# Writing each 256-column product as two runs of 128 columns, one in each half of its PSUM bank

## The chip, the core and the metric

The kernel runs on one core of one Trainium2 chip. The metric is the device time of one execution in microseconds (us), where lower is better. Five engines work side by side and wait for each other through semaphores: PE (TensorE; its weight loads are listed apart as PEld), DVE (VectorE), ACT (ScalarE), POOL (GpSimd), and SP, from which most transfers are issued.

## The reference

The input x has 2048 tokens of 512 features. It is normalised by rows, then goes through a Fourier mixing branch and a two-layer network, and the two are multiplied:

```python
xn = _layernorm(x)
a = einsum("bsd,ed->bse", xn, dft_hid_re);  b = einsum("bsd,ed->bse", xn, dft_hid_im)
s = einsum("ts,bse->bte", dft_seq_re, a) - einsum("ts,bse->bte", dft_seq_im, b)
h = relu(einsum("bsd,df->bsf", xn, w1) + b1) ** 2        # 512 -> 1792
g = silu(einsum("bsf,fd->bsd", h, w2) + b2)              # 1792 -> 512
return x + s * g
```

All data are float32.

## The kernel before, in words

**Numbers.** Every float32 operand is split into a high and a low part of type fp32r (`split`, L125 on ACT and L128 on DVE), and each product of two tiles is three matmuls: high by high, high by low, low by high (`PASSES`).

**Blocks.** Matrices are cut into 2x2 blocks, and a block product is done with seven products in place of eight (`PRODUCTS`); the sums of blocks that this needs are made on DVE. The seven products are added up either inside PSUM (units, below) or by DVE when they leave it (`combine`, L306).

**PSUM.** There are eight banks of 512 float32 columns on 128 partitions. A tile from `bank` is one whole bank.

**Stages, in order of time.**

- *Plain part of the Fourier mixing's first stage* (`products`, L340): matmuls with 512 moving columns, whose output fills a bank from column 0 to 511.
- *The rest of that stage* (`mm`, L325): 48 steps of seven products, 2016 matmuls with 256 moving columns. The moving operand lies in the buffers `ga` and `gb`, the weights in `xc0` to `xc7`. The output of a matmul goes to two runs of 128 columns, one in each half of the bank: the bank is seen as `p (i d t)` with i=2, d=2, t=128, and a matmul writes all of i and t at one d. The matmul for d=0 writes columns 0 to 127 and 256 to 383, the one for d=1 the rest.
- *y's second stage* (`YUnit`, L705): 8 units of seven products of 12 matmuls, 672 in all. It multiplies by the hidden-dimension matrices.
- *MLP1* (`HUnit`, L705): 28 units of seven products of 6 matmuls, 1176 in all.
- *MLP2* (`outer`, L811): 28 steps of seven products of 6 matmuls, 1176 in all: four token chunks (c) of seven steps (p). The moving operand W2[p] lies in `wd1`, `ga`, `gb`, `xc2`, `xc3`, `xc0`, `xc1` for p = 0 to 6; the weights g come from `xc6`, `xc7` and `xc4`, the last of them from `wd0`.

**A unit** of the y stage or of MLP1 has four regions, A to D, each the first 256 columns of a bank of its own (`region`, L702). Products 1 and 2 add up in A; ACT copies A with the sign turned into B after product 1 (`seed`), where 6, 5 and 3 are added; B goes likewise into C after product 6, where product 4 is added; 7 stands alone in D. ACT takes D, A and the last state of B out (`m7`, `c11`, `c12`), DVE takes B and C out (`c22`, `c21`). Products of one unit are placed between those of the unit before, so that PE has others to do while a region is read.

**In MLP2** the 256 columns of the two token halves i=0 and i=1 go to columns 0 to 255 and 256 to 511 of the product's bank. DVE adds the seven banks of a chunk up with `combine` (for the last chunk with `step` at the end of the program), ACT writes the bias into three banks ahead (`bias`).

**Order.** The order of instructions on each engine is that of the program text (the scheduling is manual), with small tables (`Y_SIDE`, `H_SIDE`, `O_SIDE`, `EARLY`) that say between which products the loads, sums and splits of later operands are recorded. Neither order nor tables are touched here. Most loads are issued from SP, the stores of h and y from ACT's queue.

Of the kernel before, what the change touches and what calls it, by code (L numbers as in the profile page):

```python
# [10 lines left out]
AF = mybir.ActivationFunctionType  # L11
ALU = mybir.AluOpType

P = 128
S, D, F = 2048, 512, 1792
# [72 lines left out]
HI, LO = 0, 1  # L88
# [23 lines left out]
H_SLOT = {S3: 0, S1: 1, S2: 2, S4: 3, A12: 4, A11: 5, A22: 6}  # L112

C21, C11, C22, C12 = range(4)
# [5 lines left out]
def fnet_gated_kernel(ctx, tc, x, xt, ct, wd, w1, w2, b1, b2, out):  # L120
    nc = tc.nc
# [12 lines left out]
    def copy(to, src, scale=1.0):  # L134
        nc.scalar.activation(to, src, AF.Copy, scale=scale)
# [5 lines left out]
    b1s = pool.tile([P, NF], F32, name="b1s")  # L141
    b2s = pool.tile([P, D], F32, name="b2s")
# [12 lines left out]
    def bank(tag, name):  # L155

        return acc.tile([P, 512], F32, tag=tag, name=name)
# [8 lines left out]
    def halves(ap):  # L166
        return ap.rearrange("p (a b) -> p a b", a=2)


    XC = [buf(f"xc{j}", [P, 7, 2, 256], f"xc{j}", F32R) for j in range(NJ)]  # L170

# [122 lines left out]
            for q, v in ((slice(0, 3), slice(1, 4)), (slice(3, 7), slice(4, 8))) if apart else ((slice(0, 7), slice(1, 8)),):  # L294
                split(g[:, HI, q], g[:, LO, q], u[:, v])

    def combine(part_, ms):

        for to, m, frm, op in ((C21, 1, None, None), (C11, 2, C21, ALU.add), (C22, 6, C21, ALU.add),
                               (C21, 7, C22, ALU.subtract), (C12, 5, C22, ALU.subtract), (C22, 5, C21, ALU.add),  # L300
                               (C12, 3, C12, ALU.add), (C21, 4, C21, ALU.subtract)):
            m = ms[m].rearrange("p (i n) -> p i n", i=2)
            if frm is None:
                copy(part_(to), m)
            else:
                nc.vector.tensor_tensor(part_(to), m, part_(frm), op=op)  # L306
            yield
# [11 lines left out]

    def mm(ps, w, mv, first, last):  # L320

        ps = ps.rearrange("p (i d t) -> p d i t", i=2, d=2)
        for d in range(2):
            for a_, b_ in PASSES:
                nc.tensor.matmul(ps[:, d], w[:, a_, d * P:(d + 1) * P], halves(mv(b_)),  # L325
                                 start=first and d == 0 and (a_, b_) == (HI, HI),
                                 stop=last and (a_, b_) == (LO, HI), skip_group_check=True)
# [216 lines left out]
    for n, s in enumerate(steps):  # L544
# [5 lines left out]
        for p in FIRST if j == 0 and c > PLAIN else ORDER:  # L550
# [4 lines left out]
            a, b = PRODUCTS[p]  # L555
# [16 lines left out]
        if j == NJ - 1:  # L572
            e = buf("e", [P, 2048], f"c{c}")
# [9 lines left out]
    xT, W1, W2, fin, ready = {}, {}, {}, {}, {}  # L583
# [105 lines left out]
    class Unit:  # L689
# [5 lines left out]
        def region(self, k):  # L695
            if k not in self.at:
                tag = ("bb", "b20", "ba", "b21"), ("bc", "b30", "b32", "b31")
                self.at[k] = bank(tag[self.n % 2]["ABCD".index(k)], f"r{self.n}_{k}")[:, 0:256]
            return self.at[k]

        def products(self, *ks):
            for k in ks:  # L702
                ops = list(self.operands(PRODUCTS[k]))
                for i, (w, mv) in enumerate(ops):
                    nc.tensor.matmul(self.region(REGION[k]), w, mv, start=i == 0 and k in (1, 7),  # L705
                                     stop=i == len(ops) - 1, skip_group_check=True)

        def seed(self, to, frm):
            copy(self.region(to), self.region(frm), -1.0)

        def m7(self):
            copy(self.out(C21), self.region("D"))

        def c22(self):
            nc.vector.tensor_tensor(self.out(C22), self.region("B"), self.out(C21), op=ALU.add)  # L715

        def c21(self):
            nc.vector.tensor_tensor(self.out(C21), self.region("C"), self.out(C21), op=ALU.subtract)

    class YUnit(Unit):  # L720

# [11 lines left out]
            return self.y[:, k in (C21, C22), (k in (C12, C22)) * 256:][:, 0:256]  # L733

        def c11(self):
            copy(self.out(C11), self.region("A"))

        def square(self):
            pass

        def c12(self):
            copy(self.out(C12), self.region("B"))
            n = 2 * self.n * P
            nc.scalar.dma_start(Y[n // TC][n % TC:n % TC + 2 * P].rearrange("(h p) e -> p h e", h=2), self.y)

# [2 lines left out]
    class HUnit(Unit):  # L748
# [14 lines left out]
            nc.scalar.activation(to, frm, AF.Relu, bias=b1s[:, f:f + 1])  # L763

        def c11(self):
            self.relu(self.out(C11), self.region("A"), 0)

        def c12(self):
            self.relu(self.out(C12), self.region("B"), 0)
            if self.n in ACT_PAIR:  # L770
                self.relu(self.out(LOWER), self.out(LOWER), 1)

        def lower(self, to, frm, op):
            f = 2 * (self.n % NP) + 1
            nc.vector.scalar_tensor_tensor(self.out(to), self.region(frm), b1s[:, f:f + 1], self.out(C21),
                                           op0=ALU.add, op1=op)

        def c22(self):
# [18 lines left out]
    BIASED = {2: 0, 5: 1, 4: 0}  # L797

    def bias(m, n, cols=slice(0, 2)):

        m = m.rearrange("p (k e) -> p k e", k=2)[:, cols]
        b = BIASED[n] * 256
        copy(m, b2s[:, None, b:b + 256].to_broadcast([P, cols.stop - cols.start, 256]))

    def outer(m, k, n, cols=(0, 1)):

        p = n % NP
        a, b = PRODUCTS[k]
        for i in cols:
            for a_, b_ in PASSES:  # L810
                nc.tensor.matmul(m[:, i * 256:(i + 1) * 256], ready[n][:, a_, H_SLOT[a], i * P:(i + 1) * P],  # L811
                                 W2[p][:, b_, b], start=p == 0 and i == 0 and (a_, b_) == (HI, HI) and k not in BIASED,
                                 stop=p == NP - 1 and (a_, b_) == (LO, HI), skip_group_check=True)


# [161 lines left out]
    for n in range(NTC * NP):  # L977
        c, p = divmod(n, NP)
        last = c == NTC - 1
        if n and not last and p == 0:  # L980

            ms = Banks(c)
            for k in (2, 4, 5):
                bias(ms[k], k)
        elif last and p == 0:

            ms = {k: bank(t, f"m{k}_last") for k, t in
                  {1: "b20", 2: "b21", 6: "b30", 7: "b31", 5: "bb", 3: "ba"}.items()}
            m4 = bank("bc", "m40_last"), bank("b32", "m41_last")
            bias(ms[5], 5)  # L990
            bias(m4[0], 4, slice(0, 1))
            bias(ms[2], 2)
            bias(m4[1], 4, slice(1, 2))

        def add(k, p):
            if last and k == 4:
                for i in range(2):
                    outer(m4[i], k, NP * c + p, (i,))
            else:
                outer(ms[k], k, NP * c + p)  # L1000

        go(*O_SIDE.get(n, ((), ()))[0])
        if n == 1:
            for k, i in ((1, 1), (2, 1), (6, 1), (4, 1), (5, 0), (3, 0), (7, 1), (5, 1), (3, 1)):
                add(k, i)
        elif n and (not last or p < REST):
            for k in ORDER if p else FIRST_LAST if last else FIRST:
                add(k, p)
        if n == 1:

            nc.scalar.activation(stats[:, 0, 0, 0:1], stats[:, 0, 0, 0:1], AF.Silu)
        if not n:
            go("h2")
        go(f"h{n + 3}")
        if p == NP - 1 and not last:
            e = buf("e", [P, 4, 512], f"z{c}")
            list(combine(lambda k: halves(e[:, k]), ms))
            done_next = c, e
        if c and not last and p in (3, 4):
            put(*done, p - 1)  # L1020
        go(*[f"h{n + 2}"][:n], *O_SIDE.get(n, ((), ()))[1], f"h{n + 6}")
        if p == (3 if last else 5):
            load_fin(c)
        if p == NP - 1 and not last:
            done = done_next
        elif c:
            for k in ((2, 3), (0,), (1,), (), (), (), ())[p] if not last else ((), (0,), (1,), (2,), (3,), (), ())[p]:
                finish(*done, k)
# [1 line left out]

    e = buf("u", [P, 4, 512], f"z{c}")
    tail = NP - 1
    whole = slice(0, 512)
    w = [slice(i * 256, (i + 1) * 256) for i in range(2)]

    def rest(ks, ps=range(REST, NP)):
        for k in ks:
            for f in ps:
                add(k, f)

    def step(to, a, b, op, w=whole):
        nc.vector.tensor_tensor(e[:, to, w], a[:, w], e[:, b, w], op=op)

    for f in range(REST, tail - 1):
        rest((1, 2, 6, 7, 5), (f,))
    rest((1, 2), (tail - 1,))
    rest((1, 2), (tail,))
    nc.scalar.activation(e[:, C21], ms[1], AF.Copy)
    step(C11, ms[2], C21, ALU.add)
    silu(e, C11)  # L1050
    for f in (tail - 1, tail):
# [3 lines left out]
    add_x(c, e, C11)  # L1055
    step(C21, ms[7], C12, ALU.subtract)
    rest((5,), (tail - 1, tail))
    for i in range(2):
        nc.vector.tensor_tensor(m4[i][:, w[i]], m4[i][:, w[i]], e[:, C21, w[i]], op=ALU.subtract)
    step(C22, ms[5], C21, ALU.add)  # L1060
    silu(e, C22)
    step(C12, ms[5], C12, ALU.subtract)
# [8 lines left out]
    for i, part_ in enumerate((one, two)):  # L1071
        for f in range(REST, NP):
            outer(m4[i], 4, NP * c + f, (i,))
        nc.scalar.activation(e[:, C21, w[i]], m4[i][:, w[i]], AF.Silu)
        times(c, e, C21, part_)
        plus(c, e, C21, part_)

# [42 lines left out]
```

## Time and profile before

| what | before |
|---|---|
| time, median of 3 runs (lowest to highest) | 702.24 us (702.05 to 703.04) |
| the profiled execution's own time | 701.75 us |
| its span, first to last instruction | 700.0 us |
| mean granted TensorE clock over the span | 0.998 |
| ACT busy | 357.9 us (51%), 475 instructions |
| HBM traffic over the span | 214 GB/s |

The views that the prediction shows are the page's busy times, its clock row, groups of instructions by line, the chain of waits in order of time, and windows. In a group's row stand the line, engine and operation, then output<-inputs, then shapes; behind the count x, the busy time of the group in us and the mean length of one in ns. Since matmuls overlap, the length of one (280 ns) isn't the time that each adds. That time is read from the chain of waits: a row there has its start in us, its length in us, the engine, the tile, the line and how many instructions it holds, and rows don't overlap, so length by count is what one matmul added. In a window's row stand the two ends, the length, and for each engine the busy us in it with the count of instructions, then the granted clock, the share of DMA and GB/s.

### The profile page before, as it was taken

How to read it: one execution, taken by the hardware profiler on the slowest of the kernel's cores; microseconds unless marked ns; L12 is line 12 of the kernel's file. 1: busy time of each engine (PE TensorE's matmuls, PEld its weight loads, DVE VectorE, ACT ScalarE, POOL GpSimd, SP SyncE). 2: the span in 40 equal slices, each digit the busy share in tenths (PEclk: the TensorE clock that was granted, in tenths of full speed). 3: DMA queues.
4: the chain of work that ended last, by engine and by line, in shares of the span. 5: the costliest groups of instructions: out<-in, count | busy, mean ns of one | idle time of the engine just before them, and what ended most of it. 6: DMA issues, size and time to landing. Idle time of an engine off the chain costs nothing.

```text
span 700.0 us, 13144 instructions
## 1 busy us (share of the span) xinstructions
PE 693.0 (99%) x5440; PEld 670.1 (96%) x5440; DVE 605.6 (87%) x849; ACT 357.9 (51%) x475; POOL 6.4 (1%) x9
## 2 busy tenths in 40 slices
PE   8999999999999999999999999999999999999997
PEld 5778889999999999999999999999999999999997
DVE  7999769999999898788899788899748689989896
ACT  4436544435343343435455358777778764444451
POOL 0000000000000000000000000000000000101000
PEclk9999999999999999999999999999999999999999
DMA  8535756768486754367488457587426956767745
GB/s 298 198 104 197 257 202 219 257 204 290 158 294 211 259 210 166 121 239 274 151 287 280 151 185 287 195 322 266 154 118 197 388 168 188 194 197 195 227 155 157
DMA packets 51723, 150.82 MB, mean 215 GB/s; under 512 B 4944, under 2 KB 19536, under 8 KB 50256
## 3 DMA queue, kind: packets, MB, share of 16 engines
q1 hardware_dynamic: 44096, 129.80, 54.9%
q10 hardware_dynamic: 6208, 18.88, 6.8%
q0 software_dynamic: 1360, 1.31, 1.5%
q8 instruction: 42, 0.69, 0.4%
q14 instruction: 17, 0.14, 0.1%
HBM read 101.98 MB, written 47.99 MB: 214 GB/s over the span
## 4 chain that ended last, share of the span: by engine, by line
PE 94%; DVE 3%; DMA 1%; ACT 1%; issue 1%; SPq 0%; DVEq 0%; ACTq 0%
PE m L325 33%; PE m_o L811 15%; PE r_B L705 13%; PE r_A L705 8%; PE pq_b L340 8%; PE r_C L705 4%; PE r_D L705 4%; PE m_last L811 4%; PE pq_ba L340 2%; PE pq_bc L340 1%; PE pq_bb L340 1%; DMA rows<-rows 1%; DVE yg L128 0%; DMA x<-in_x 0%; DVE bn L185 0%
## 5 line engine op out<-in xcount | busy, mean ns | idle before, releaser
L325 PEld LDWEIGHTS m<-g,xc 128*128 128x128 f32 x2016 | 235.7, 188 | 0.6 <-DVE g L128 0.2
L325 PE MATMUL m<-g,xc 128*128 128x256 f32 x2016 | 236.2, 280 | 0.0
L125 ACT ACTIVATE g<-u 128x1792 fp32r<-128x1792 f32 (+3 forms) x70 | 100.1, 1431 | 143.2 <-PE m L325 47.7
L128 DVE TENSOR_TENSOR g<-u,g 128x1792 fp32r<-128x1792 f32 (+3 forms) x70 | 117.5, 1679 | 23.3 <-ACT g L125 23.1
L811 PE MATMUL m_o<-w,g 128*128 128x256 f32 x882 | 105.7, 282 | 0.0
L811 PEld LDWEIGHTS m_o<-w,g 128*128 128x128 f32 x882 | 105.5, 191 | 0.0
L125 ACT ACTIVATE g<-hr 128x1792 fp32r<-128x1792 f32 (+2 forms) x31 | 47.9, 1556 | 47.2 <-PE m_o L811 25.2
L705 PE MATMUL r_B<-xT,w 128*128 128x256 f32 x504 | 69.4, 282 | 0.0
L340 PE MATMUL pq_b<-g,xc 128*128 128x512 f32 x240 | 66.7, 397 | 1.1 <-ACT xc L125 1.0
L705 PEld LDWEIGHTS r_B<-xT,w 128*128 128x128 f32 x504 | 64.1, 190 | 0.0
L128 DVE TENSOR_TENSOR g<-hr,g 128x1792 fp32r<-128x1792 f32 (+2 forms) x31 | 56.7, 1837 | 7.1 <-ACT g L125 7.1
L340 PEld LDWEIGHTS pq_b<-g,xc 128*128 128x128 f32 x240 | 43.8, 188 | 13.9 <-ACT xc L125 3.1
L705 PE MATMUL r_A<-xT,w 128*128 128x256 f32 x336 | 44.7, 282 | 0.0
L705 PEld LDWEIGHTS r_A<-xT,w 128*128 128x128 f32 x336 | 42.1, 190 | 0.0
L705 PE MATMUL r_B<-wdp,yg 128*128 128x256 f32 x288 | 37.5, 283 | 0.2 <-DVE y L715 0.2
L705 PEld LDWEIGHTS r_B<-wdp,yg 128*128 128x128 f32 x288 | 35.6, 190 | 0.6 <-DVE y L715 0.4
L811 PE MATMUL m_last<-w,g 128*128 128x256 f32 x294 | 35.1, 282 | 0.0
L811 PEld LDWEIGHTS m_last<-w,g 128*128 128x128 f32 x294 | 35.1, 190 | 0.0
L257 DVE TENSOR_TENSOR u<-u 128x512 f32<-128x512 f32 x48 | 32.8, 684 | 1.7 <-DMA u<-in_ct 1.7
L128 DVE TENSOR_TENSOR yg<-yraw,yg 128x1792 fp32r<-128x1792 f32 x13 | 26.2, 2021 | 5.4 <-ACT yg L125 5.4
L306 DVE TENSOR_TENSOR c<-m,c 128x512 f32<-128x512 f32 x42 | 27.2, 684 | 1.7 <-PE m L325 1.0
L125 ACT ACTIVATE yg<-yraw 128x1792 fp32r<-128x1792 f32 x13 | 22.1, 1699 | 7.2 <-DVE yraw L266 5.5
(180 smaller groups left out, 862.7 us busy)
## 6 DMA issues: line engine op xcount, KB each, us to landing
u<-in_ct SPq DMA_DIRECT2D x63, 512.0 KB, 3.7
hd<-h ACTq DMA_DIRECT2D x28, 512.0 KB, 4.8
hr<-hd SPq DMA_DIRECT2D x28, 512.0 KB, 3.9
wdp<-wdd SPq DMA_DIRECT2D x8, 896.0 KB, 7.2
yraw<-pqd SPq DMA_DIRECT2D x13, 512.0 KB, 5.0
pqd<-c SPq DMA_DIRECT2D x6, 1024.0 KB, 4.4
w<-w1d SPq DMA_DIRECT2D x6, 896.0 KB, 8.7
y<-y ACTq DMA_DIRECT2D x8, 512.0 KB, 4.1
```

The costliest lines, as they stand in the source:

```text
L125: nc.scalar.activation(hi, src, AF.Copy)
L128: nc.vector.tensor_tensor(lo, src, hi.bitcast(F32), op=ALU.subtract)
L257: nc.vector.tensor_tensor(t[:, 0:2], r[:, 0:1].to_broadcast([P, 2, 256]), r[:, 1:3], op=ALU.add)
L306: nc.vector.tensor_tensor(part_(to), m, part_(frm), op=op)
L325: nc.tensor.matmul(ps[:, d], w[:, a_, d * P:(d + 1) * P], halves(mv(b_)), start=first and d == 0 and (a_, b_) == (HI, HI), stop=last and ( ...
L340: nc.tensor.matmul(accs[c][k], w, part[c, j][:, b_, 2 * h:2 * h + 2], start=j == 0 and h == 0 and (a_, b_) == (HI, HI), stop=j == NJ - 1 a ...
L705: nc.tensor.matmul(self.region(REGION[k]), w, mv, start=i == 0 and k in (1, 7), stop=i == len(ops) - 1, skip_group_check=True)
L811: nc.tensor.matmul(m[:, i * 256:(i + 1) * 256], ready[n][:, a_, H_SLOT[a], i * P:(i + 1) * P], W2[p][:, b_, b], start=p == 0 and i == 0 an ...
```

## The change

Matmuls of y's second stage, of MLP1 and of MLP2 write their 256 columns in the way that L325 does. A helper `spread` gives the view of a bank with its two halves (i), two places in each (k) and 128 columns (t). A unit's region is place k=0: columns 0 to 127 and 256 to 383 of its bank. In MLP2 token half i=0 takes place 0 and i=1 place 1. All that reads or writes these banks follows: copies, seeds, sums, biases and activations see the same 256 or 512 numbers as two or four runs of 128. Buffers in SBUF keep their layout (`halves`, `packed`). `mm` uses `spread` too, for the view it had.

```diff
+    def spread(m):
+        return m.rearrange("p (i k t) -> p k i t", i=2, k=2)
+    def packed(z):
+        return z.rearrange("p (k i t) -> p k i t", k=2, i=2)
...
-    def combine(part_, ms):
+    def combine(part_, ms, view=halves):
...
-            m = ms[m].rearrange("p (i n) -> p i n", i=2)
+            m = view(ms[m])
...
-        ps = ps.rearrange("p (i d t) -> p d i t", i=2, d=2)
+        ps = spread(ps)
...
-                self.at[k] = bank(tag[self.n % 2]["ABCD".index(k)], f"r{self.n}_{k}")[:, 0:256]
+                self.at[k] = spread(bank(tag[self.n % 2]["ABCD".index(k)], f"r{self.n}_{k}"))[:, 0]
...
-                    nc.tensor.matmul(self.region(REGION[k]), w, mv, start=i == 0 and k in (1, 7),
+                    nc.tensor.matmul(self.region(REGION[k]), w, halves(mv), start=i == 0 and k in (1, 7),
...
-            copy(self.out(C21), self.region("D"))
+            copy(halves(self.out(C21)), self.region("D"))
...
-            nc.vector.tensor_tensor(self.out(C22), self.region("B"), self.out(C21), op=ALU.add)
+            x_ = halves(self.out(C21))
+            nc.vector.tensor_tensor(halves(self.out(C22)), self.region("B"), x_, op=ALU.add)
...
-        m = m.rearrange("p (k e) -> p k e", k=2)[:, cols]
+        m = spread(m)[:, cols]
...
-                nc.tensor.matmul(m[:, i * 256:(i + 1) * 256], ready[n][:, a_, H_SLOT[a], i * P:(i + 1) * P],
-                                 W2[p][:, b_, b], start=p == 0 and i == 0 and (a_, b_) == (HI, HI) and k not in BIASED,
+                nc.tensor.matmul(spread(m)[:, i], ready[n][:, a_, H_SLOT[a], i * P:(i + 1) * P],
+                                 halves(W2[p][:, b_, b]), start=p == 0 and i == 0 and (a_, b_) == (HI, HI) and k not in BIASED,
...
-            list(combine(lambda k: halves(e[:, k]), ms))
+            list(combine(lambda k: packed(e[:, k]), ms, spread))
...
-    def step(to, a, b, op, w=whole):
-        nc.vector.tensor_tensor(e[:, to, w], a[:, w], e[:, b, w], op=op)
+    def step(to, a, b, op):
+        nc.vector.tensor_tensor(packed(e[:, to]), spread(a), packed(e[:, b]), op=op)
```

The other edits do the same to `c21`, `c11`, `c12`, `lower` and to the last chunk's copies, subtractions and activation.

No instruction is added, removed or moved on any engine. PE's order at a product of MLP1, before (the regions are r_A to r_D, xT is the moving operand, w the weights):

```order
L705 MATMUL r_A<-xT_5010,w_5_4626 128x256 x3
L705 MATMUL r_A<-xT_5206,w_5_4626 128x256 x3
L705 MATMUL r_A<-xT_5010,w_6_4535 128x256 x3
L705 MATMUL r_A<-xT_5206,w_6_4535 128x256 x3
L705 MATMUL r_B<-xT_5010,w_5_4626 128x256 x3
```

The same rows with the change, whose line number is 7 higher:

```order
L712 MATMUL r_A<-xT_5010,w_5_4626 128x2x128 x3
L712 MATMUL r_A<-xT_5206,w_5_4626 128x2x128 x3
L712 MATMUL r_A<-xT_5010,w_6_4535 128x2x128 x3
L712 MATMUL r_A<-xT_5206,w_6_4535 128x2x128 x3
L712 MATMUL r_B<-xT_5010,w_5_4626 128x2x128 x3
```

Only the shape of the output has changed, from one run of 256 to two of 128.

More of the change, by code (lines that the diff above doesn't have):

```diff
@@ L711, in m7 @@
         def m7(self):
-            copy(self.out(C21), self.region("D"))
+            copy(halves(self.out(C21)), self.region("D"))
         def c22(self):
-            nc.vector.tensor_tensor(self.out(C22), self.region("B"), self.out(C21), op=ALU.add)
+            x_ = halves(self.out(C21))
+            nc.vector.tensor_tensor(halves(self.out(C22)), self.region("B"), x_, op=ALU.add)
         def c21(self):
-            nc.vector.tensor_tensor(self.out(C21), self.region("C"), self.out(C21), op=ALU.subtract)
+            x_ = halves(self.out(C21))
+            nc.vector.tensor_tensor(x_, self.region("C"), x_, op=ALU.subtract)
     class YUnit(Unit):
@@ L735, in c11 @@
         def c11(self):
-            copy(self.out(C11), self.region("A"))
+            copy(halves(self.out(C11)), self.region("A"))
         def square(self):
@@ L741, in c12 @@
         def c12(self):
-            copy(self.out(C12), self.region("B"))
+            copy(halves(self.out(C12)), self.region("B"))
             n = 2 * self.n * P
@@ L765, in c11 @@
         def c11(self):
-            self.relu(self.out(C11), self.region("A"), 0)
+            self.relu(halves(self.out(C11)), self.region("A"), 0)
         def c12(self):
-            self.relu(self.out(C12), self.region("B"), 0)
+            self.relu(halves(self.out(C12)), self.region("B"), 0)
             if self.n in ACT_PAIR:
@@ L774, in lower @@
             f = 2 * (self.n % NP) + 1
-            nc.vector.scalar_tensor_tensor(self.out(to), self.region(frm), b1s[:, f:f + 1], self.out(C21),
+            nc.vector.scalar_tensor_tensor(halves(self.out(to)), self.region(frm), b1s[:, f:f + 1], halves(self.out(C21)),
                                            op0=ALU.add, op1=op)
@@ L799, in bias @@
     def bias(m, n, cols=slice(0, 2)):
-        m = m.rearrange("p (k e) -> p k e", k=2)[:, cols]
+        m = spread(m)[:, cols]
         b = BIASED[n] * 256
-        copy(m, b2s[:, None, b:b + 256].to_broadcast([P, cols.stop - cols.start, 256]))
+        copy(m, halves(b2s[:, b:b + 256])[:, None].to_broadcast([P, cols.stop - cols.start, 2, P]))
     def outer(m, k, n, cols=(0, 1)):
@@ L1032, in fnet_gated_kernel @@
     tail = NP - 1
-    whole = slice(0, 512)
-    w = [slice(i * 256, (i + 1) * 256) for i in range(2)]
     def rest(ks, ps=range(REST, NP)):
@@ L1047, in fnet_gated_kernel @@
     rest((1, 2), (tail,))
-    nc.scalar.activation(e[:, C21], ms[1], AF.Copy)
+    copy(packed(e[:, C21]), spread(ms[1]))
     step(C11, ms[2], C21, ALU.add)
@@ L1057, in fnet_gated_kernel @@
     rest((5,), (tail - 1, tail))
+    left = [spread(m4[i])[:, i] for i in range(2)]
     for i in range(2):
-        nc.vector.tensor_tensor(m4[i][:, w[i]], m4[i][:, w[i]], e[:, C21, w[i]], op=ALU.subtract)
+        nc.vector.tensor_tensor(left[i], left[i], packed(e[:, C21])[:, i], op=ALU.subtract)
     step(C22, ms[5], C21, ALU.add)
@@ L1073, in fnet_gated_kernel @@
             outer(m4[i], 4, NP * c + f, (i,))
-        nc.scalar.activation(e[:, C21, w[i]], m4[i][:, w[i]], AF.Silu)
+        nc.scalar.activation(packed(e[:, C21])[:, i], left[i], AF.Silu)
         times(c, e, C21, part_)
```

## The prediction

> **What bounds the kernel now.** I read the page's busy times and clock first, then what PE waited for, then the chain of waits.
>
> ```profile
> PE 693.0 (99%) x5440; PEld 670.1 (96%) x5440; DVE 605.6 (87%) x849; ACT 357.9 (51%) x475; POOL 6.4 (1%) x9
> ...
> PEclk9999999999999999999999999999999999999999
> ...
> PE 94%; DVE 3%; DMA 1%; ACT 1%; issue 1%; SPq 0%; DVEq 0%; ACTq 0%
> ...
> PE warm L443 <- DVE idle L439: 1.2, 1, 1.2
> PE pq_b L340 <- ACT xc L125: 1.0, 1, 1.0
> PE r_B L705 <- DVE y L715: 0.2, 1, 0.2
> ```
>
> PE is busy 99% of the span at a full clock, 94% of the chain that ended last is PE, and PE waited 2.4 us in all. So the time is the number of matmuls by what each adds, and the question is whether the change alters that. The chain of waits in order of time gives it (start, length, matmuls), in stretches where nothing but matmuls stands on it:
>
> ```profile
> 109.97 31.03 PE m L325 x266
> 184.88 30.22 PE m L325 x259
> 595.10 10.02 PE m_o L811 x85
> 605.35 19.68 PE m_o L811 x164
> 630.19 9.90 PE m_o L811 x84
> ```
>
> Those are stretches asked for one by one; the next rows are of the whole chain.
>
> ```profile
> 53.26 2.10 PE pq_b L340 x9
> ...
> 356.38 2.87 PE r_B L705 x24
> ...
> 396.51 2.87 PE r_B L705 x24
> ...
> 430.85 1.44 PE r_B L705 x12
> ...
> 545.97 1.44 PE r_B L705 x12
> ...
> 557.37 103.11 PE m_o L811 x864
> 660.48 27.15 PE m_last L811 x228
> ```
>
> L325 already writes in two runs: 31.03/266 = 116.7 ns a matmul, and 30.22/259 = 116.7 again. The three stages that the change touches write one run of 256 columns, with the same shapes, and are slower:
>
> - y's second stage: units of 84 matmuls begin alike at 356.38 and, four units on, at 396.51: 40.13 us/336 = 119.4 ns.
> - MLP1: units of 42 begin alike at 430.85 and, 23 on, at 545.97: 115.12/966 = 119.2 ns. The stretches shown run at 1.44/12 = 120.0.
> - MLP2: 103.11/864 = 119.3, and 27.15/228 = 119.1 for the last chunk. Within it, 19.68/164 = 120.0 and 10.02/85 = 9.90/84 = 117.9.
>
> So 3024 of the 5440 matmuls take 2 to 3 ns more than L325's. The groups say that this isn't one bad place: the mean lengths differ too, for weight loads and matmuls.
>
> ```profile
> L325 PEld LDWEIGHTS m<-g,xc 128*128 128x128 f32 x2016 | 235.7, 188 | 0.6 <-DVE g L128 0.2
> L325 PE MATMUL m<-g,xc 128*128 128x256 f32 x2016 | 236.2, 280 | 0.0
> L811 PE MATMUL m_o<-w,g 128*128 128x256 f32 x882 | 105.7, 282 | 0.0
> L811 PEld LDWEIGHTS m_o<-w,g 128*128 128x128 f32 x882 | 105.5, 191 | 0.0
> ```
>
> **The change part by part.** *The matmuls.* 672 + 1176 + 1176 = 3024 get the output view of L325; nothing else about them changes. Whether the view is what makes L325 faster must be argued, since L325 also reads other buffers. The best comparison is inside the trace. MLP2's steps p=1 and p=2 take the moving operand from `ga` and `gb` and the weights from `xc` tiles, which is where L325 has them. A step is 42 matmuls, so the second chunk's p=1 and p=2 are the 84 matmuls from 595.1, the third's those from 630.2: 117.9 ns. Same buffers, same sizes, one run instead of two: 1.2 ns more than 116.7. The steps behind them, p=3 to p=6, take the moving operand from `xc` tiles as well: 120.0. So about 1.2 ns of the 3.3 stands against the write pattern with the buffers held alike, and 2.1 goes with where the moving operand lies. What two runs do at 120.0 no row shows. The bounds: they remove nothing there, or they bring all matmuls to 116.7. Against a gain beyond the 1.2 speaks L340, which writes 512 columns in one piece at 2.10/9 = 233 ns, 116.7 per 256 columns, without any broken run; but it has half as many weight loads per column, and it too passes from one half of a bank to the other every 256 columns, which units do never and MLP2 only every third matmul. I take the upper bound, 116.7 everywhere, because it is the one value that all 2016 broken writes and all stretches of L325 show, with no second level, while the unbroken ones move between 117.9 and 120.0.
>
> *What of it lies on the path.* At the start of the y stage the chain comes onto PE for good at 347.52, and at the end it leaves PE at 687.63:
>
> ```profile
> 347.52 1.69 PE r_B L705 x12
> ...
> 679.97 7.66 PE m_last L811 x64
> ```
>
> Unit 0 of the y stage and the first 24 matmuls of unit 1 stand before 347.52, so 564 of the 672 count; in MLP2 the last 66 run beside DVE's final sums. The sum:
>
> - y: 564 x (119.4 - 116.7) = 1.5 us
> - MLP1: 1176 x (119.2 - 116.7) = 2.9 us
> - MLP2: 864 x (119.3 - 116.7) + 228 x (119.1 - 116.7) = 2.2 + 0.5 = 2.8 us (the 18 that stand among MLP1's last products add under 0.1)
>
> together 7.2 us.
>
> *The evictions.* About 85 ACT and 100 DVE instructions read or write the banks in runs of 128. The nearest rows:
>
> ```profile
> L135 ACT ACTIVATE r_C<-r_B 128x256 f32<-128x256 f32 x36 | 13.5, 374 | 9.3 <-PE r_B L705 8.8
> L135 ACT ACTIVATE plain<-pq_b 128x512 f32<-128x512 f32 x4 | 2.3, 593 | 4.4 <-PE pq_b L340 4.4
> L135 ACT ACTIVATE z<-m_o 128x512 f32<-128x512 f32 x3 | 1.8, 597 | 12.0 <-PE m_o L811 12.0
> L718 DVE TENSOR_TENSOR h<-r_C,h 128x256 f32<-128x256 f32 x9 | 3.8, 424 | 1.8 <-PE r_C L705 1.6
> L306 DVE TENSOR_TENSOR z<-m_o,z 128x512 f32<-128x512 f32 x21 | 13.7, 688 | 3.5 <-PE m_o L811 3.1
> ```
>
> `plain` is written in runs of 128 and takes 593 ns where the unbroken z takes 597: runs cost nothing. That is the lower bound, 0. The upper one is that each further run pays the fixed part again: on ACT 374 - (597 - 374) = 151 ns, on DVE 424 - (688 - 424) = 160 ns. What hides it:
>
> ```profile
> 421.00:551.00 130.00, 130.00 (x1093) 130.00 (x1092) 104.55 (x154) 99.46 (x191) 0.00 (x0) 1.00 0.65 232
> 583.00:609.00 26.00, 26.00 (x220) 26.00 (x220) 24.75 (x33) 12.70 (x13) 2.55 (x2) 1.00 0.72 195
> ```
>
> In MLP1 (first row) a unit of 5.0 us has 4.0 us of DVE and 3.8 us of ACT (130 us hold 26 units). Two more runs on DVE and five on ACT make it 4.3 and 4.6, under the 4.9 us that a faster unit has; with 2.1 us of other products between a read of B and the next write to it, PE still waits for none. The tight place is the border between two chunks of MLP2 (second row), where DVE has 24.75 of 26 us: the faster PE does those matmuls in 26 x 116.7/119.3 = 25.4 us, so DVE just fits, and with seven sums of four runs in place of one (up to 7 x 3 x 0.16 = 3.4 us) it would not, by some 2.7 us at each of two borders. Behind the last matmuls nothing hides DVE: six sums there would add 6 x 3 x 0.16 = 2.9 us. So the give-back is 0 to 8.3 us; being nearest to the row of `plain`, I take 0.4 us, for waits that the tighter beat alone makes at the borders (an estimate).
>
> Total: 7.2 - 0.4 = 6.8 us. The profiled execution goes from 701.75 to 694.9, and the median, 0.5 us above it, from 702.24 to about 695.4.
>
> **The rivals.** *Where the operands lie decides, and the runs matter only off the 120.0 level.* For it: the two levels inside MLP2 with one write pattern. Then the 1.2 ns falls on the matmuls that are below 120.0 now. From the mean, (120.0 - 119.3)/(120.0 - 117.9) = a third of MLP2, and by the means of 119.2 and 119.4 as much or a little more of the other two: 1000 x 1.2 = 1.2 us, 701.0. If it is additive at every level, 3024 x 1.2 = 3.6 us, 698.6. Against: nothing in the trace shows two runs at the slow places. Chance of an outcome between these, 0.20.
>
> *No change.* The three stages stay at 119 to 120 ns, and the difference of 1.2 ns is due to how L325 lays out the high and low parts of its weights, which also differs from MLP2's: 702.2. Chance 0.13.
>
> *Slower: a broken write costs.* At each matmul the second run begins anew, on PE's way into PSUM. L325's 116.7 speaks against it; for it, that no row shows two runs together with operands at the 120.0 level, where one more hold-up isn't covered. As a price I take the step between levels, 1.2 ns, on all: 3024 x 1.2 = 3.6 us, 705.9; it decides as soon as the stages run above 120.0. DVE's dearer sums (at most 8.3 us) come out on the same side only near their upper bound, or where the matmuls gain nothing. Chance 0.22. The Trainium skill ("PSUM — Partial Sum Buffer", Specifications) states this rival as a rule: PSUM has lines of 8 bytes, and any access pattern that isn't contiguous slows matmuls significantly. By that rule read literally the change loses on all 3024; in this trace the 2016 matmuls of L325 with the broken pattern are the fastest of their size, so the rule doesn't hold for runs of 128 columns there.
>
> **How the numbers follow.** The forecast, 116.7 ns in all three stages, has 0.45: 695.4. Alone it reaches from 694.3 (no give-back, a little more at the ends) to 697.5 (a third of the give-back's bound). The range takes in the rivals up to no change and a small loss, 694.2 to 703.6. About 0.2% (1.4 us) can be told from no change. Faster by more: 0.45 and most of the 0.20, 0.63. Within: 0.13 and the smallest of the partial gains, 0.15. Slower: 0.22.
>
> **What would show it.** In the profile after, the groups of the three stages should show matmuls of 280 and weight loads of 188 ns, and the chain stretches in MLP2 of 9.8 us for 84 matmuls from `ga` and `gb` and the same per matmul, 116.7, behind them. 120.0 left at p=3 to p=6 would prove the first rival. Evictions: 374, 597, 424 and 688 ns as before; over 500 ns for 256 elements would bring the give-back. PE's waits should stay under 4 us; if DVE's z sums become what PE waits for, the give-back was taken too low. The forecast is wrong if any of the three stages stays above 118.5 ns.

## The result, and the profile after

| | before | changed | ratio, 95% interval |
|---|---|---|---|
| median | 702.44 us (12 runs) | 702.60 us (12 runs) | 1.0002 [0.9993, 1.0011] |
| profiled execution: its own time, span | 701.75, 700.0 us | 702.87, 701.1 us | |

The change made no difference that can be measured. The page of the changed kernel first (busy times, clock, the chain's shares), then what PE waited for:

```profile
PE 693.9 (99%) x5440; PEld 670.9 (96%) x5440; DVE 605.7 (86%) x849; ACT 358.1 (51%) x475; POOL 6.4 (1%) x9
...
PEclk9999999999999999999999999999999999999999
...
PE 93%; DVE 4%; DMA 1%; ACT 1%; issue 1%; SPq 0%; DVEq 0%; ACTq 0%
```

```profile
PE warm L450 <- DVE idle L446: 1.2, 1, 1.2
PE pq_b L347 <- ACT xc L125: 1.0, 1, 1.0
PE r_B L712 <- DVE y L723: 0.2, 1, 0.2
```

PE is as busy as before and waits for the same three things, for the same 2.4 us. The whole chain of waits of the changed kernel (start, length, matmuls):

```profile
357.45 2.87 PE r_B L712 x24
...
397.58 2.87 PE r_B L712 x24
...
431.92 1.44 PE r_B L712 x12
...
547.04 1.44 PE r_B L712 x12
...
558.44 103.11 PE m_o L820 x864
661.55 27.16 PE m_last L820 x228
```

Compare the differences of starts with those in the prediction. Four units of the y stage: 397.58 - 357.45 = 40.13 us, before 40.13. Twenty-three units of MLP1: 115.12, before 115.12. MLP2: 103.11 and 103.11 again. The three stages that the change rewrote take what they took, to a hundredth of a microsecond. Each of their rows stands 1.07 us later than before (357.45 against 356.38, 431.92 against 430.85, 558.44 against 557.37), so the 1.1 us by which this span is longer arose ahead of them, in code that does what it did: L325's stage, now L332. Stretches of the changed kernel's chain tell how:

```profile
150.00 31.03 PE m L332 x266
189.92 25.09 PE m L332 x213
299.97 30.12 PE m L332 x258
595.08 9.92 PE m_o L820 x84
605.36 19.66 PE m_o L820 x164
```

The first stage runs at 31.03/266 = 116.7 ns a matmul, then at 25.09/213 = 117.8, then at 30.12/258 = 116.7 again. By the starts of its matmuls it changes level at about 181 and 300 us, each time at the border of a chunk (eight steps of this stage, some 39 us), and nowhere between. Some 1010 matmuls by 1.1 ns are the 1.1 us. **117.8 is therefore a level that L325's own form, two runs, can have.** The last two rows are MLP2 with two runs: 118.1 for p=1 and p=2 (117.9 before; the count rounds by one in 84) and 119.9 behind them (120.0 before).

Groups of the changed kernel, matmuls and evictions:

```profile
L332 PEld LDWEIGHTS m<-g,xc 128*128 128x128 f32 x2016 | 236.7, 188 | 0.7 <-DVE g L128 0.5
L332 PE MATMUL m<-g,xc 128*128 128x256 f32 x2016 | 237.2, 279 | 0.1
...
L820 PE MATMUL m_o<-w,g 128*128 128x256 f32 x882 | 105.7, 282 | 0.0
L820 PEld LDWEIGHTS m_o<-w,g 128*128 128x128 f32 x882 | 105.5, 191 | 0.0
...
L313 DVE TENSOR_TENSOR z<-m_o,z 128x512 f32<-128x512 f32 x21 | 13.7, 688 | 3.8 <-PE m_o L820 3.4
L135 ACT ACTIVATE r_C<-r_B 128x256 f32<-128x256 f32 x36 | 13.5, 374 | 9.0 <-PE r_B L712 8.6
```

MLP2 keeps 282 and 191 ns, where the forecast wanted 280 and 188. The evictions keep 688 and 374 ns to the nanosecond, now in runs of 128.

### The profile page after: what moved, and what is told of

The parts are those of the page before. It is cut to its first block, busy times and chain, and to the rows that moved or that the text cites. A ratio compares the mean times of both kernels' runs of the same rounds, so it can differ in the third digit from the quotient of the medians.

```text
span 701.1 us, 13144 instructions
## 1 busy us (share of the span) xinstructions
PE 693.9 (99%) x5440; PEld 670.9 (96%) x5440; DVE 605.7 (86%) x849; ACT 358.1 (51%) x475; POOL 6.4 (1%) x9
## 4 chain that ended last, share of the span: by engine, by line
PE 93%; DVE 4%; DMA 1%; ACT 1%; issue 1%; SPq 0%; DVEq 0%; ACTq 0%
PE m L332 32%; PE m_o L820 15%; PE r_B L712 13%; PE r_A L712 8%; PE pq_b L347 8%; PE r_C L712 4%; PE r_D L712 4%; PE m_last L820 4%; PE pq_ba L347 2%; PE pq_bb L347 1%; PE pq_bc L347 1%; DVE c L313 1%; DVE g L128 1%; DMA rows<-rows 1%; DVE yg L128 0%
## 5 line engine op out<-in xcount | busy, mean ns | idle before, releaser
L332 PEld LDWEIGHTS m<-g,xc 128*128 128x128 f32 x2016 | 236.7, 188 | 0.7 <-DVE g L128 0.5
L332 PE MATMUL m<-g,xc 128*128 128x256 f32 x2016 | 237.2, 279 | 0.1
```

## The experiments

In what follows a matmul's *step* is the time from its start to the next one's. Steps come in levels, and the trace's starts show them: in long stretches 113, 113, 114, over and over (113.3), or 117 to 119 (117.8). *Distance* is the start of the moving operand in SBUF less that of the weights, modulo 256 bytes. It follows from the order in which buffers are allocated: every large one holds a whole multiple of 256 bytes (14336 for most), and each buffer of the small tile `sm` between them takes 32. In the kernel before, the first stage and MLP2's steps p=1 and p=2 have distance 32; MLP2's other steps have 0, but for the very last, whose weights lie in `wd0` (224); MLP1 has 0 or 224. In the y stage three matmuls at 32 and nine at 0 take turns, so that only means over whole units say something there.

**One run in the first stage** asks directly whether the view matters: the stage that was fastest gets the view that was blamed, and the three later stages stay as before.

```diff
-        ps = ps.rearrange("p (i d t) -> p d i t", i=2, d=2)
+        ps = ps.rearrange("p (d n) -> p d n", d=2)
...
-                nc.tensor.matmul(ps[:, d], w[:, a_, d * P:(d + 1) * P], halves(mv(b_)),
+                nc.tensor.matmul(ps[:, d], w[:, a_, d * P:(d + 1) * P], mv(b_),
...
```

The rest of the edit makes the sums behind them read the banks so.

> The kernel before, with the first stage's matmuls (L325) writing one run of 256 columns in place of two, and the sums behind them reading it so. Theory A (the time per matmul is a level that depends on how weight loads and moving reads meet, not on the output view): the stage stays between 116.7 and 117.8 ns per matmul, the time within 0.2% of 702.4 us. Theory B (two runs are what makes this stage faster, and something in the later stages hides it there): the stage goes to 117.9 to 120 ns, 2016 x 1.2 to 3.3 ns = 2.4 to 6.7 us slower.

Measured: 702.14 us against 702.39, ratio 0.9999 [0.9990, 1.0009]. In the first stage the mean step was 117.6 ns: 116.7 up to 142 us, 117.8 behind it. A stretch of its chain from either side:

```profile
108.95 11.08 PE m L325 x95
149.94 29.09 PE m L325 x247
```

11.08/95 = 116.6 and 29.09/247 = 117.8. So one run has the same two levels as two runs. Of the difference that the forecast was built on, this stage shows nothing that belongs to the view.

**Both kernels again.** One more profiled execution of each.

> The kernel before, unchanged. Theory A2 with two levels at a distance of 32 bytes (116.7 and 117.8 ns, which of them being left to the short stalls at the chunk borders of the first stage): the first stage's mean lies anywhere from 116.7 to 117.8, not at 116.68 again, and changes only at a border; the y stage, MLP1 and MLP2 repeat their means of 119.4, 119.1 and 119.2 within 0.1. Rival: the level is a property of the program, and the first stage repeats 116.7 throughout.

> The changed kernel, unchanged. The same two theories: a first stage that changes between 116.7 and 117.8 ns only at chunk borders and at others than in its first profile, or one that repeats 116.7 up to 181 us, 117.8 up to 300 and 116.7 behind.

Two stretches of the kernel before, in this second profile of it:

```profile
189.97 25.09 PE m L325 x215
229.94 25.09 PE m L325 x213
```

116.7 and 117.8: the kernel before has both levels too. Its first profile was at 116.7 from the start of the stage to its end. The kernel after had 117.8 from 108 to 222 us this time, and 116.7 elsewhere. Single times: 702.44 and 703.33 us.

**Where the operands start.** The first form of the theory took the starts modulo 64 bytes: operands that start alike step at 120.0, others lower. Three placements, by a byte count of small tiles alone. All large buffers at multiples of 64:

```diff
-    eps = pool.tile([P, 1], F32, name="eps")
+    eps = pool.tile([P, 16], F32, name="eps")[:, 0:1]
...
-        t = root[j] = buf("sm", [P, 4], f"root{j}_{hs.start}")
+        t = root[j] = buf("sm", [P, 16], f"root{j}_{hs.start}")
```

> The kernel before, with two small tiles made larger so that all large SBUF buffers begin at multiples of 64 bytes (before: the xc buffers and wd1 begin 32 bytes past one, ga, gb and wd0 at one). Theory A in the form 'the level goes by the start addresses of the two reads': the stages with weights and moving operand both 32 past (120.0 ns) leave that level; if the 32 bytes are the cause, all stages run at about 116.7 ns and the time is about 695 us; if two equal remainders are the cause, all run at 120 and it is about 709. Theory C (other engines' and transfers' traffic in the later stages sets the level): no change, 702.4 us.

The second of these edits alone, by which all lie 32 bytes past a multiple of 64:

> The kernel before, with one small tile made larger so that ga, gb and wd0 too begin 32 bytes past a multiple of 64, as the xc buffers do. Theory A by addresses: the first stage (L325) goes from 116.7 to 120.0 ns, 2016 x 3.3 = 6.7 us, MLP2's steps with ga and gb go from 117.9 to 120.0 as well, 0.7 us: about 709.8 us. Theory C: no change, 702.4 us.

The first alone, by which the `xc` tiles and `wd1` lie at multiples of 64 and `ga`, `gb` and `wd0` 32 past them:

> The kernel before, with one small tile made larger so that the remainders change places: xc buffers and wd1 at multiples of 64 bytes, ga, gb and wd0 32 past. Theory A by addresses: the first stage (weights at 0, moving operand at 32) leaves 116.7; the nearest row is MLP1 with weights in ga and gb, 118.3 ns, so about 3 us slower there; MLP2's steps with both in xc run as all stages of the run with all at 64 do. Theory C: no change, 702.4 us.

Measured: 705.47 us (1.0046 [1.0031, 1.0061]), 706.99 (1.0067 [1.0049, 1.0084]) and 702.32 (1.0001 [0.9991, 1.0010]). Placement alone moves the time, which the view did not, but not as modulo 64 has it. In the first two a stretch of the first stage reads (one row of each):

```profile
189.97 25.04 PE m L325 x211
```

```profile
189.99 25.04 PE m L325 x211
```

Both 118.7 ns, not 120.0, and in the third the first stage keeps 116.7 with few at 117.8. Modulo 256 all three fall in line: in the first stage the distance is 128 in the first two and 32, as before, in the third.

**Unequal placement, with either view.** The buffers that follow `xc0` to `xc3` are shifted by 8 elements, so that in all stages nearly all operands start unequal modulo 64; once in the kernel before, once in the changed one.

```diff
+    SHIFTED = "xc0", "xc1", "xc2", "xc3"
...
+        return buf(tag, [P, 3600], name, F32R)[:, 8:3592].rearrange("p (a s n) -> p a s n", a=2, s=7)
...
```

> The kernel before (one run of 256 columns), with the operands so placed that in all stages the moving operand and the weights begin at different remainders of 64 bytes: the late tenants of xc0 to xc3 begin 32 bytes further on, wd1 at a multiple of 64. Theory A (the level of time per matmul goes by whether the two remainders are equal): the 677 matmuls of MLP1 and 795 of MLP2 that are at 119.7 and 119.9 ns go to the 118.3 and 117.9 that their unequal neighbours have, 1.0 + 1.6 us, the y stage gains at most 0.5 us: 699 to 700 us. If the levels reach 116.7 everywhere it is 695. Theory C (traffic of other engines and transfers): no change, 702.4 us.

> The changed kernel (two runs in all stages) with the same placing as e5. Theory A: the same as e5 within 0.2%, the three stages' time per matmul the same within 0.3 ns. Theory B in its weaker form (two runs help only where the operands lie well): faster than e5, by up to 3024 x 1.2 = 3.6 us.

Measured: 700.95 us (0.9979 [0.9970, 0.9988]) and 700.94 (0.9980 [0.9971, 0.9989]). The three later stages step at 118.1, 117.8 and 117.9 ns in both, in place of 119.4, 119.1 and 119.3; the first stage rose to 118.4, since its distances became 32, 96, 160 and 224. MLP2 with one run, then with two:

```profile
559.89 40.22 PE m_o L822 x341
```

```profile
559.90 40.10 PE m_o L831 x340
```

117.9 in both. So the view has no part off the 120.0 level either, which was what the rival "where the operands lie" had left for it. Within these stretches the distances differ from step to step. The first chunk's p=5, whose moving operand lies in the shifted `xc0`, has distance 32; one run, then two:

```profile
580.55 4.67 PE m_o L822 x40
```

```profile
580.55 4.67 PE m_o L831 x40
```

By the starts of the 42 matmuls both step at 116.7. So matmuls of MLP2 with one run can stand at the very level that the forecast gave to two runs.

**Distance 32 in the first stage, the y stage and six of MLP2's seven steps; distance 0 everywhere.** The first shifts five buffers by 8 elements and moves small tiles between the large ones (MLP1 stays at 224 or 0 in six of its seven steps); the second takes one small tile away:

```diff
-        bufs = {"u": 3, "bn": 3, "sm": 3}.get(tag, 1)
+        bufs = {"u": 3, "bn": 3, "sm": 2}.get(tag, 1)
```

> The kernel before (one run of 256 columns) with the buffers so placed that the moving operand begins 32 bytes past the weights' start, counted modulo 256 bytes, in the first stage, in the y stage, in six of seven steps of MLP2 and in one of seven steps of MLP1; the other steps of MLP1 and MLP2 are at 224 or 0. Theory A2 (the level goes by that distance modulo 256: 116.7 or 117.8 ns at 32, 118.3 at 224, 120.0 at 0 and 96, from the runs so far): MLP2 2.4 us, y 1.6 us, MLP1 1.3 us faster, the first stage as before: about 697 us (696 to 698.5). Theory A1 (only equal or unequal modulo 64): as e5, 701 us.

> The kernel before with one small buffer fewer (two turns of 'sm' in place of three), which puts ga, gb and wd0 32 bytes lower: the distance of moving operand and weights is 0 modulo 256 in all stages. Theory A2: the first stage goes to 120.0 ns, 2016 x 3.3 = 6.7 us slower, MLP2's steps with ga and gb to 120.0 too, 0.7 us: about 709.5 us. Theory A1 (modulo 64, where e2 and e3 had 118.7 in the first stage): 705.5 to 707 us.

Measured: 698.98 us (0.9956 [0.9943, 0.9968]) and 709.12 (1.0099 [1.0083, 1.0114]). The first came 2 us above what was expected, because its matmuls stood partly at 117.8 and not at 116.7, as mean steps of 117.0 in the first stage and 117.6 in MLP2's steps at distance 32 show. The second came as expected. Its first stage and its MLP2, with distance 0:

```profile
149.98 29.04 PE m L325 x242
```

```profile
599.95 50.16 PE m_o L811 x418
```

120.0 in both: the fastest stage of the kernel became as slow as the slowest, with its broken write left as it was. Its weights, with high and low parts side by side in each slot, and MLP2's, with all high parts ahead, cost the same here.

**Distances 64 and 192**, by `"sm": 4` and `"sm": 8` in the line above:

> The kernel before with one small buffer more (four turns of 'sm'), so that ga, gb and wd0 lie 32 bytes higher: the distance in the first stage and in MLP2's steps with ga and gb is 64 modulo 256, in MLP1's steps with weights there 192. Theory A2: between its neighbours 32 (116.7 to 117.8) and 96 (120.0), some 118 to 119 ns in the first stage: 2016 x 1.3 to 2.3 = 2.6 to 4.7 us slower, 705 to 707 us. Theory A1 (modulo 64, remainders equal): 118.7 ns, 706 us.

> The kernel before with five small buffers more, ga, gb and wd0 160 bytes higher: the distance in the first stage is 192 modulo 256, in MLP1's steps with weights there 64. Theory A2: between its neighbours 160 (118.9 in this stage) and 224 (118.3), some 118.3 to 118.9 ns: 3.3 to 4.5 us slower, 705.7 to 707 us. Theory A1 (remainders equal): 118.7 ns, the same as at 128 and 64.

Measured: 703.10 us (1.0011 [1.0002, 1.0021]) and 696.53 (0.9913 [0.9887, 0.9939]). Both were expected slower; the second has the wrong sign. I had taken 64 and 192 to lie between what their neighbours showed, 118 to 119, and they have two levels, 113.3 and 117.8. With 64 nearly all of the first stage fell on 117.8, with 192 about half. In the run with 192, the first two rows are the first stage, the third MLP2's p=1 and p=2 (distance 192), the fourth p=3 to p=6 (distance 0):

```profile
109.92 10.09 PE m L325 x89
189.95 10.13 PE m L325 x86
591.66 9.08 PE m_o L811 x80
605.98 20.04 PE m_o L811 x167
```

113.4, 117.8, 113.5 and 120.0 ns. The last two are one stage, one view, one run of the program, with 6.5 ns between them. In its y stage three matmuls at 192 and nine at 0 take turns; two units on the chain:

```profile
375.19 2.84 PE r_B L705 x24
...
385.13 2.84 PE r_B L705 x24
```

9.94 us for 84 matmuls are 118.3 ns, which is what a quarter at 113.3 and three quarters at 120.0 make.

**Distance 64 or 192 in all stages.** By now it was open whether the later stages, where the forecast had failed, follow the same law throughout, and whether the view counts for something at 113.3. The `xc0` to `xc3` and `wd1` buffers of later stages are shifted by 16 elements, small tiles fill the rest; once with the view of before, once with that of the change.

```diff
+    SHIFT = {"xc0": 16, "xc1": 16, "xc2": 16, "xc3": 16, "wd1": 16}
...
+    def factor(tag, name, off=None):
+        off = SHIFT.get(tag, 0) if off is None else off
+        return buf(tag, [P, off + 3584], name, F32R)[:, off:].rearrange("p (a s n) -> p a s n", a=2, s=7)
...
```

> The kernel before, with the buffers placed so that in all stages the moving operand starts 64 or 192 bytes past the weights, modulo 256. Theory (the distance sets which levels a matmul can run at): at 192 and 64 the earlier runs had two levels, 113.3 and 117.8 ns, in the first stage and in MLP2's steps from ga and gb. If the law holds in the later stages as well, each of them lies between 113.3 and 117.8 in place of 119.1 to 119.4 now: with both levels taken half of the time 5040 matmuls by 115.6 ns, about 689 us; the ends are 680 (113.3 throughout) and 699 (117.8 throughout). Rival (the later stages are slow for a reason of their own, such as shorter runs of one accumulation or one bank): they stay at 117 to 119.4, MLP1 above 118.5, and the time is above 697.

> The same placement with the changed kernel's two runs of 128 columns. Theory (the output view plays no part at any level): the same levels, 113.3 and 117.8, and a time within 1% of the run beside it, the rest being which of the two levels a stretch falls on. Rival (two runs help or cost once the matmuls run at 113): a level that the run with one piece of 256 does not show, 1.2 ns higher or lower on 3024 matmuls, 3.6 us.

Measured: 688.64 us (0.9809 [0.9793, 0.9826]) with one run, 688.33 (0.9805 [0.9790, 0.9820]) with two. Rows of the whole chain of the first of them, MLP1:

```profile
425.70 1.36 PE r_B L719 x12
...
430.46 1.36 PE r_B L719 x12
```

A unit of 42 takes 430.46 - 425.70 = 4.76 us, 113.3 ns a matmul, where it took 5.0. Two stretches of MLP2 with one run, p=2 and p=3 (distance 64), then p=4 (192); and the first of them with two runs:

```profile
588.79 9.66 PE m_o L825 x82
598.80 4.43 PE m_o L825 x39
```

```profile
588.76 9.66 PE m_o L834 x82
```

117.8, 113.6, and 117.8 with two runs. Mean steps over whole stages, one run against two: MLP1 113.65 and 113.65, MLP2 116.16 and 116.19, y 117.18 and 117.21, first stage 114.28 and 114.27. So MLP1 and MLP2 have the levels of the first stage at these distances, and the view is worth nothing at any level seen here. The y stage, where 64 and 192 take turns every three matmuls, lies between the two levels in both runs. Both kernels beat the two that this study began with, by some 13.5 us.

What the gain turns into next stands on the page of the one with one run: the share of the chain.

```profile
PE 81%; DVE 13%; ACT 2%; issue 2%; DMA 1%; ACTq 0%; DVEq 0%
```

DVE stood on the chain for 3% before. PE now runs ahead of it at the borders of chunks and in the last chunk of MLP2, so the next nanosecond taken from a matmul should be worth less; no run tested that.

The levels of the first stage, of MLP2 and, at 0, 64 and 192, of MLP1, in stretches or as means over at least 117 matmuls:

| distance, bytes | step, ns | seen in |
|---|---|---|
| 0 | 120.0 | first stage, MLP1, MLP2 |
| 32 | 116.7 or 117.8 | first stage, MLP2 |
| 64 | 113.3 or 117.8 | first stage, MLP1, MLP2 |
| 96 | 119.9 to 120.1 | first stage, MLP2 of the unequal placement |
| 128 | 118.7 to 118.9 | first stage, MLP2 |
| 160 | 117.4 (MLP2), 118.9 (first stage) | the unequal placement |
| 192 | 113.3 or 117.8 | first stage, MLP1, MLP2 |
| 224 | 118.3 | first stage, MLP2 of the unequal placement |

Means over MLP1's matmuls at the other distances are near these: 116.8 at 32, 119.6 at 96, 118.6 at 128, 119.0 at 160 and 118.3 at 224. That the distance counts modulo 256, and not 512, can be seen in the run with distance 0 everywhere: modulo 512 its first stage has 256 and MLP2's p=3 to p=6 have 0, and both step at 120.0. Modulo 128 would not do, since 0 and 128 differ (120.0 against 118.7).

## Why the prediction was wrong

**What bounds the kernel** was right: PE is 99% busy at a full clock, and every kernel here whose mean step changed clearly moved its time the same way.

**The step that failed** is the comparison inside the trace: "Same buffers, same sizes, one run instead of two: 1.2 ns more than 116.7." The 117.9 of MLP2's p=1 and p=2 and the 116.7 of L325 are the two levels of one distance, 32, and not two views. L325 with two runs shows 117.8 in the changed kernel, and with one run shows both; MLP2 with one run shows 116.7 in the unequal placement. The buffers were the same, but the state that a stretch had fallen into was not, and I had nothing that held it fixed.

**What made it look safe** is the next step: 116.7 "is the one value that all 2016 broken writes and all stretches of L325 show, with no second level". That was true of the one execution that I had, from the first of these matmuls to the last. A second execution of the same kernel has the other level in plain sight (25.09/213). The steps of the slower stages did not vary between executions, so nothing there warned that L325's could. What could have warned stood in MLP2: 117.9 and 120.0 with one view show that something other than the view sets levels, and I let the view explain the rest. The whole 7.2 us stands on this step; measured gain in the three stages: 0.0.

**The 2.1 ns** that I gave to "where the moving operand lies" is the half that was right. What counts is where it lies against the weights, as the run with distance 0 everywhere shows: there `ga` and `gb` give 120.0 too.

**The evictions** were right, at the lower bound: 688 ns for the sums of z and 374 for the seeds, as before. So the further runs cost nothing that these means show on DVE or ACT, and the give-back of 0.4 us had nothing to follow from, since the beat did not tighten.

**The rivals.** *Where the operands lie decides* named the right cause, but still gave 1.2 ns to the runs below 120.0 (698.6 to 701.0 us); the two unequal placements show 117.9 with either view. *No change* has the right time (702.2) and the wrong reason: the weights' layout plays no part at distance 0, where both layouts give 120.0. *Slower: a broken write costs* is refuted at each level: 119.9 at distance 0, 117.8 at 32 and 64, 113.3 at 192, with two runs as with one. The Trainium skill's sentence behind it ("PSUM — Partial Sum Buffer", Specifications), that a pattern that isn't contiguous slows matmuls significantly, does not hold for runs of 128 columns: 3024 matmuls were given the pattern at a ratio of 1.0002 [0.9993, 1.0011].

**The range** held the time, through the rivals; the likeliest case did not. A slip in its working changed nothing: 702.24 less 7.2 us of gain, plus a third of the 8.3 us that could be given back, is 697.8 and not 697.5.

**What stays open.** Why the distance sets the step, no run shows; it was found by moving buffers and holds over the kernels here. Nor is it settled what picks one of two levels. A level holds for tens of microseconds and changes mostly near a chunk's border, where PE is held up for up to 0.6 us, but not at each of them, and a few changes lie beside no such hold-up. In MLP2's p=1 and p=2, at distance 32, all five traces that keep the placement of before show 117.9, with one run or two; 116.7 was seen in MLP2 only where buffers had been moved. The first stage takes different levels in different executions of one kernel, and so does the time (694.13 to 697.39 us with distance 192). Distances 96, 160 and 224 were seen only in stages that mix them with others, and at 160 MLP2 disagrees with the first stage and MLP1.

## What to carry to other kernels

Before a difference between two groups of like instructions is given to the one thing by which their code differs, look whether either group alone has two values, over its whole length and in a second execution: a change of 1 ns in 117 was here a state and not a cause. When matmuls of one shape step differently, look at where their operands start against each other, modulo 256 bytes; here moving the starts of buffers by tens of bytes was worth 13.5 us, and the written view nothing. An experiment that takes the supposed cause away from the fast case (one run in the first stage) settles more than one that gives it to the slow case.

## What was not expected of the hardware

- A matmul of 256 columns with its weight load steps at 113.3 to 120.0 ns, 6%, with its SBUF distance, at a granted clock of 0.998 to 1.0 in all runs.
- The weight load's recorded length tells distance 0 from others: its mean is 192 ns in all four stages of the run with distance 0 everywhere, 188 in those of the runs with distances 64 and 192 in all stages, and 188 in the first stage at 32 and at 128 too, whose steps differ by 2 ns.
- At distances 32, 64 and 192 there are two levels (116.7 or 117.8, 113.3 or 117.8), and one execution of an unchanged program differs from the next in which of them its first stage is at.
